# Indirect transfers spread over unit and expert steps, and two more slots turned by the transposing transfer, in a fused attention and mixture-of-experts kernel

## The chip, the cores and the metric

The kernel runs on one core of one Trainium2 chip. The metric is the time of the device in microseconds (us); lower is better.

## What is computed

Eight batches of 576 tokens with eight heads of 64 go through masked attention. The first four heads see a window of 32 tokens, the last four see every 32nd token. The result, 4608 tokens of 512 numbers, goes through a top-1 mixture of eight experts, each with a hidden layer of 1024. All numbers are float32.

```python
scores = scale * np.matmul(q, k.transpose(0, 1, 3, 2))
scores = np.where(masks, scores, -1e9)          # local for heads 0-3, strided for 4-7
attn = softmax(scores)
x = (attn @ v) as [4608, 512]
logits = x @ w_gate + modality_bias[modality_id]
e_idx = argmax(logits)
for e in range(8):
    h = np.maximum(x[e_idx == e] @ w1[e], 0.0)
    out[e_idx == e] = gate_w * (h @ w2[e])
```

## The kernel before, in words

**Attention, 0 to about 170 us.** Batches are taken in four pairs. Each pair has eight units, alternately a local head and a strided half, 32 units in all. A loop over n (line 1044) does one stage of several units in each turn: scores of unit n, transposes of n-2, masks of n+1, values of n-3. TensorE's order there is the order of the code. When a pair is complete, `finish_pair` and `route` (lines 465 to 605) turn its results, write the token rows to DRAM (`xd`), compute the router and write an entry for each token (`ld`), ordered by expert. They are generators, and `pop` runs five of their pieces per turn.

**Slots.** Tokens of one expert are handled in slots of 384. There are 12 slots that always run and one half slot. `slots(ph)` makes, on VectorE, tables of which rows belong to which slot (`li`, line 714) and which weights they need (`wi`, line 723). It runs three times, after the second, third and fourth pair. The first table serves slots 0 and 1, the second slots 2 and 3, the third slots 4 to 11.

**What a slot fetches.** Everything goes through GpSimd's (POOL's) indirect transfers, in POOL's order: three look-ups `le` (128 entries each, line 771), three gathers `fx` (128 token rows each, line 759), and the weights in four quarters of 1 MB (`raw0`, `raw1` and two in `raw23`, line 786); at the end three scatters `out` (line 938). A gather needs the look-up of its part, a look-up needs the table. `in_turn` (line 745) ties each of these behind the one before, so that the scheduler keeps the order of the code.

**What a slot computes.** `ffn` (line 907) runs eight steps f. A step casts the weights (`wh` on ScalarE line 951, `wl` on VectorE line 952), does 12 matmuls into `h` (line 916), a Relu (`hh`, line 919) and its remainder (`hl`, line 921), and two steps later 9 matmuls into `o` (line 930). Weights of the next slot are loaded at f = 1, 3, 5, 7 (`WHEN`). At f = 3 the look-ups of slot k+3 are issued, at f = 4 the gathers of slot k+2.

**Turning.** The gathered tokens have to be transposed. Slots 1 to 3 (below `TURNED`, line 47) get it from TensorE: 12 transposes at f = 4 of the slot before (`turn_tokens`, line 860). Slots from 4 on get it from the transposing transfer: at f = 1 VectorE splits the rows into 16-bit planes (`plane_tokens`, line 881), at f = 3 SyncE (SP) issues three transposing transfers (`send_tokens`, line 889), and at f = 6 VectorE puts the planes together (line 899) and ScalarE and VectorE make `xh` and `xl` (lines 903, 904). The three transposing transfers wait until quarter 1 of the next slot's weights has landed (line 892), and the first gather that comes after them waits until they have landed (line 763).

## Time and profile before

| | us |
|---|---|
| median of three runs | 617.81 (616.23 to 620.71) |
| the profiled execution, whole | 611.66 |
| its span, first to last instruction | 609.9 |
| TensorE busy in it | 577.3 |
| VectorE, ScalarE, GpSimd busy | 382.7, 328.3, 191.9 |
| mean granted TensorE clock | 0.979 of full |

The span is one execution; 1.76 us lie around it. "Idle" is the time that an engine stood before an instruction, and what follows the arrow is what ended it; "issue" means that nothing in the profile accounts for the wait. TensorE's clock has two levels, 1.2 and 2.4 GHz; 1.00 in the column PEclk is 2.4 GHz, 0.50 is 1.2 GHz.

### The profile page before, as it was taken

Reading aid. Unit: us, or ns where it says so; the run is one execution under the profiler, and the core shown is the slowest. Engines: PE = TensorE matmul, PEld = TensorE weight load, DVE = VectorE, ACT = ScalarE, POOL = GpSimd, SP = SyncE. Lnnn points to the kernel's source line nnn. Section 1 sums busy time; section 2 is a strip of 40 time slices with the busy share of each in tenths; the row PEclk is TensorE's granted clock in tenths of the full one; section 3 lists DMA queues with packets and bytes.
Section 4 is the critical chain, followed back from the end, with each engine's and each line's share of the span. In section 5 each row is a group of like instructions: output and inputs, shape, how many; then the busy total and the mean of one; then the engine's idle time right before and its main releaser. Section 6 shows DMA issues by size and latency. Waiting matters only on the chain.

```text
span 609.9 us, 13599 instructions
## 1 busy us (share of the span) xinstructions
PE 577.3 (95%) x5461; PEld 509.3 (84%) x5461; DVE 382.7 (63%) x925; ACT 328.3 (54%) x656; POOL 191.9 (31%) x184
## 2 busy tenths in 40 slices
PE   8789899878899999999999999999999999999995
PEld 5677778766778889899989999989989899989985
DVE  6775976863883777454666574747666666746432
ACT  5688887655682544453544453635445454536342
POOL 3010000044207132571444343352544534313211
PEclk9999999895999899999999999999999999999999
DMA  8997998887708422755363336550413345432511
GB/s 309 286 283 247 342 294 284 271 307 237 247 13 324 148 105 87 239 194 206 127 177 126 89 121 153 176 116 10 106 50 87 75 185 124 168 71 95 180 71 56
DMA packets 53723, 103.50 MB, mean 170 GB/s; under 512 B 32595, under 2 KB 32851, under 8 KB 49556
## 3 DMA queue, kind: packets, MB, share of 16 engines
q0 software_dynamic: 14592, 52.75, 25.3%
q1 hardware_dynamic: 33780, 39.85, 22.9%
q10 hardware_dynamic: 5280, 9.94, 4.7%
q8 instruction: 45, 0.74, 0.5%
q14 instruction: 26, 0.21, 0.1%
HBM read 98.28 MB, written 19.18 MB: 193 GB/s over the span
## 4 chain that ended last, share of the span: by engine, by line
PE 76%; issue 3%; ACT 1%; DVE 1%; POOL 0%; ACTq 0%; POOLq 0%
PE o L930 33%; PE h L916 33%; PE s L323 1%; PE ss L410 1%; PE o L358 1%; PE ot L455 1%; PE xs L217 1%; PE lg L504 1%; ACT wh L951 1%; PE xt L217 1%; PE ts L217 1%; PE en L600 1%; PE t L217 1%; PE hh L841 0%; PE xl L217 0%
## 5 line engine op out<-in xcount | busy, mean ns | idle before, releaser
L952 DVE TENSOR_TENSOR wl<-raw,wh 128x512 fp32r<-128x512 f32 x192 | 125.9, 694 | 91.1 <-ACT wh L951 72.9
L951 ACT CAST wh<-raw 128x512 fp32r<-128x512 f32 x192 | 109.3, 619 | 119.9 <-PE o L930 109.9
L916 PE MATMUL h<-xh,wl 128*128 128x384 f32 x384 | 129.5, 337 | 0.0
L916 PE MATMUL h<-xl,wh 128*128 128x384 f32 x384 | 129.0, 336 | 0.0
L916 PE MATMUL h<-xh,wh 128*128 128x384 f32 x384 | 128.1, 337 | 0.0
L930 PE MATMUL o<-wh,hl 128*128 128x512 f32 x288 | 114.3, 397 | 0.7 <-issue 0.7
L930 PE MATMUL o<-wl,hh 128*128 128x512 f32 x288 | 114.2, 397 | 0.3 <-issue 0.3
L930 PE MATMUL o<-wh,hh 128*128 128x512 f32 x288 | 113.4, 394 | 1.0 <-issue 1.0
L919 ACT ACTIVATE hh<-h 128x384 fp32r<-128x384 f32 x96 | 47.1, 491 | 88.2 <-PE h L916 75.1
L921 DVE SCALAR_TENSOR_TENSOR hl<-h,hh 128x384 fp32r<-128x384 f32 x96 | 53.3, 555 | 59.4 <-ACT hh L919 57.7
L786 POOL DMA_INDIRECT raw<-in_w,wi x48 | 60.7, 1264 | 70.4 <-DVE wl L952 38.6
L916 PEld LDWEIGHTS h<-xh,wh 128*128 128x128 f32 x384 | 72.2, 188 | 4.3 <-PE xs L217 0.4
L916 PEld LDWEIGHTS h<-xl,wh 128*128 128x128 f32 x384 | 72.1, 188 | 3.2
L916 PEld LDWEIGHTS h<-xh,wl 128*128 128x128 f32 x384 | 72.0, 188 | 0.0
L938 POOL DMA_INDIRECT out<-y,le x36 | 37.1, 1032 | 107.8 <-ACT y L937 103.5
L930 PEld LDWEIGHTS o<-wh,hl 128*128 128x128 f32 x288 | 54.4, 189 | 12.4 <-issue 0.9
L930 PEld LDWEIGHTS o<-wl,hh 128*128 128x128 f32 x288 | 54.3, 189 | 10.5 <-issue 1.2
L930 PEld LDWEIGHTS o<-wh,hh 128*128 128x128 f32 x288 | 54.5, 189 | 9.9 <-issue 0.9
L759 POOL DMA_INDIRECT fx<-xd,le x36 | 36.8, 1022 | 55.7 <-DMA work<-work 44.6
L771 POOL DMA_INDIRECT le<-ld,li x36 | 35.5, 987 | 40.6 <-DVE li L714 30.5
L594 POOL TENSOR_TENSOR hv<-hb,val 128x576 f32<-128x576 bf16 x4 | 5.1, 1282 | 83.6 <-DVE hb L585 46.1
L323 PE MATMUL s<-qk,qd 128*64 128x64 f32 x576 | 23.7, 234 | 6.9 <-issue 6.2
(191 smaller groups left out, 779.4 us busy)
## 6 DMA issues: line engine op xcount, KB each, us to landing
qk<-in_qkl SPq DMA_DIRECT2D x16, 592.0 KB
vv<-in_vl SPq DMA_DIRECT2D x16, 585.0 KB
qks<-in_qks SPq DMA_DIRECT2D x16, 576.0 KB
xd<-xt ACTq DMA_DIRECT2D x8, 1024.0 KB
vs<-in_vs SPq DMA_DIRECT2D x16, 288.0 KB
xd<-xt ACTq DMA_DIRECT2D x4, 256.0 KB
raw<-in_w,wi POOLq DMA_INDIRECT x48
le<-ld,li POOLq DMA_INDIRECT x36
```

The lines of the kernel that those rows point to most:

```text
L217: nc.tensor.transpose(dst, src, ident)
L323: nc.tensor.matmul(s[64 * jj:64 * jj + 64, g, :], qd[:, i, :, :].rearrange("p b q -> p (b q)"), qk[:, 18 + i:20 + i, :].rearrange("p b q - ...
L759: ins = in_turn(nc.gpsimd.indirect_dma_start(xt[:, h, :], None, xd[0:xrows, :], IOA(ap=le[:, h, 0:1], axis=0), **bounds))
L771: in_turn(nc.gpsimd.indirect_dma_start(le[:, h, :], None, ld[0:1 + last, :], IOA(ap=li[:, s, h:h + 1], axis=0)))
L786: ins = nc.gpsimd.indirect_dma_start(raws[j].rearrange("p f c -> p (f c)"), None, a["w"], IOA(ap=wi[:, s, j:j + 1], axis=0), bounds_check= ...
L916: nc.tensor.matmul(hp, w[:, a1], x[:, c, :], start=(k == 0), stop=(k == 11))
L919: nc.scalar.activation(hh[:], hp, AF.Relu)
L921: nc.vector.scalar_tensor_tensor(hl[:], hp, 0.0, hh.bitcast(F32), ALU.max, ALU.subtract)
L930: nc.tensor.matmul(os[h], hx[:, m], w[:, 512:1024], start=(f == 0 and i == 0), stop=(f == 7 and i == 2))
L938: outs.add(in_turn(nc.gpsimd.indirect_dma_start(out, IOA(ap=le[:, h, 0:1], axis=0), y[:], None, bounds_check=NT - 1, oob_is_err=False)))
L951: nc.scalar.copy(wh[:, c], raw[:, c])
L952: nc.vector.tensor_tensor(wl[:, c], raw[:, c], wh[:, c].bitcast(F32), ALU.subtract)
```

## The change

Each indirect transfer becomes a piece of its own. While attention runs, two pieces are issued per turn of the loop, once the first table is there; in the slots one piece per step. Each piece waits (a real wait) for a recent result, called its pace: in attention the last result of the values stage, in the slots the Relu of the step before. Scatters are no longer links of the chain. Slot 1 alone is turned by TensorE; slots 2 and 3 go through the transposing transfer as well.

```diff
-FIND, GATHER = 3, 4
-TURNED = 4
+TURNED = 2
...
-    def in_turn(ins):
+    def in_turn(ins, result=False):
         if ordered:
-            if ordered[-1]:
-                tc.add_manual_dep(ins.ins, ordered[-1], behind, reason="order of transfers")
-            ordered.append(ins.ins.name)
+            for name in ordered[-1][:1 if result else None]:
+                tc.add_manual_dep(ins.ins, name, behind, reason="order of transfers")
+            if result:
+                ordered[-1].append(ins.ins.name)
+            else:
+                ordered.append([ins.ins.name])
+            after_landing(ins, pace[-1])
         return ins
...
-                    for k in range(3):
-                        yield
-                        look_up(k)
-                    for k in range(2):
-                        yield
-                        gather(k)
-                    yield
-                    for j in range(2):
-                        weights(tables[0][1], 0, j, True)
...
+    for k in range(2):
+        fetch(k, look_up)
+        fetch(k, gather)
+        if k == 0:
+            queue.extend((0, partial(load, 0, j)) for j in range(4))
...
+        if 0 in tables:
+            if not ordered:
+                ordered.append([])
+            issue(2)
         if n == nu + 1:
             turn(0)
-            for j in (2, 3):
-                load(0, j)
...
-            if k == 0 and f == 0:
-                look_up(2)
-            if f == FIND:
-                look_up(k + 3)
-            if f == GATHER:
-                gather(k + 2)
-
+            issue(1 if f > 1 or (k == 0 and f) else 2 if k == 0 else 0)
+
+        if k == 0:
+            fetch(2, look_up)
+        fetch(k + 3, look_up, range(2))
+        fetch(k + 2, gather, range(1))
+        fetch(k + 3, look_up, range(2, 3))
+        fetch(k + 2, gather, range(1, 3))
```

In the rows that follow, the digit behind a name is the table, and the next one the slot of that table: `le2_0` is the look-up of slot 4, `fx1_1` the gather of slot 3, `h0_17` step 7 of slot 1, `h1_00` step 0 of slot 2.

GpSimd in the last third of attention, before: both first quarters of slot 0's weights, all look-ups and all gathers of slots 0 and 1 stand together.

```order
L786 DMA raw0_2515<-in_w,wi0_2389 128x2048
L786 DMA raw1_2519<-in_w,wi0_2389 128x2048
L771 DMA le0_0_2395<-ld_88,li0_2380 128x2 x3
L771 DMA le0_1_2399<-ld_88,li0_2380 128x2 x3
L759 DMA fx0_0_2493<-xd_87,le0_0_2395 128x512 x3
L759 DMA fx0_1_2504<-xd_87,le0_1_2399 128x512 x3
L786 DMA raw23_3294<-in_w,wi0_2389 128x2048 x2
L594 TENSOR_TENSOR hv2_3033<-hb2_3031,val2_2854 128x576
```

And in the changed kernel:

```order
L794 DMA le0_0_2395<-ld_88,li0_2380 128x2 x3
L777 DMA fx0_0_2489<-xd_87,le0_0_2395 128x512 x3
L809 DMA raw0_2728<-in_w,wi0_2389 128x2048
L809 DMA raw1_2732<-in_w,wi0_2389 128x2048
L597 TENSOR_TENSOR hv2_3028<-hb2_3026,val2_2839 128x576
L809 DMA raw23_2844<-in_w,wi0_2389 128x2048 x2
L794 DMA le0_1_2939<-ld_88,li0_2380 128x2 x3
L554 COPY val3_3511<-rt_sb_85 128x9
L777 DMA fx0_1_3031<-xd_87,le0_1_2939 128x512 x3
```

The weights of slot 0 moved behind its gathers, and the last two quarters and everything of slot 1 moved behind the router's product `hv2`.

GpSimd in slot 1, before: quarter 1 of slot 2's weights (`raw1` with `wi1`) stands ahead of the look-ups that need the third table `li2`.

```order
L786 DMA raw0_2515<-in_w,wi1_3225 128x2048
L938 DMA out_0<-y0_00_3928,le0_0_2395 4608x512
L938 DMA out_0<-y0_01_3933,le0_0_2395 4608x512
L938 DMA out_0<-y0_02_3938,le0_0_2395 4608x512
L786 DMA raw1_2519<-in_w,wi1_3225 128x2048
L771 DMA le2_0_4004<-ld_88,li2_3871 128x2 x3
L759 DMA fx1_1_4066<-xd_87,le1_1_3554 128x512 x3
L786 DMA raw23_3294<-in_w,wi1_3225 128x2048 x2
```

And in the changed kernel:

```order
L809 DMA raw0_2728<-in_w,wi1_3232 128x2048
L963 DMA out_0<-y0_00_3931,le0_0_2395 4608x512
L963 DMA out_0<-y0_01_3936,le0_0_2395 4608x512
L963 DMA out_0<-y0_02_3941,le0_0_2395 4608x512
L794 DMA le2_0_3969<-ld_88,li2_3871 128x2
L809 DMA raw1_2732<-in_w,wi1_3232 128x2048
L794 DMA le2_0_3969<-ld_88,li2_3871 128x2
L777 DMA fx1_1_4045<-xd_87,le1_1_3516 128x512
```

One look-up with `li2` now stands between the scatters and quarter 1.

VectorE in the changed kernel, from the Relu remainder of slot 1's step 6 to the tokens of slot 2 (`work1_0`, `xl1_0`):

```order
L946 SCALAR_TENSOR_TENSOR hl0_16_4115<-h0_16_4100,hh0_16_4113 128x384
L714 TENSOR_TENSOR row2_3859<-row2_3859,rt2_3860 128x60
L716 TENSOR_TENSOR rt2_3860<-r2_3857,sel2_3851 128x60
L717 SCALAR_TENSOR_TENSOR li2_3871<-row2_3859,rt2_3860 128x60
L977 TENSOR_TENSOR wl1_01_4208<-raw0_2728,wh1_01_4207 128x512 x2
L946 SCALAR_TENSOR_TENSOR hl0_17_4161<-h0_17_4146,hh0_17_4159 128x384
L977 TENSOR_TENSOR wl1_02_4261<-raw1_2732,wh1_02_4260 128x512 x2
L977 TENSOR_TENSOR wl1_03_4298<-raw1_2732,wh1_03_4297 128x512 x2
L922 COPY work1_0_3919<-work1_0_3919 128x1536 x2
L927 TENSOR_TENSOR xl1_0_4120<-work1_0_3919,xh1_0_4119 128x768 x2
```

Before, `li2` stood ahead of the remainder of step 5, and no `work1_0` was there.

## Rows read from the trace of the kernel before

**Rows 1.** Windows by stage: length; busy PE, PEld, DVE, ACT, POOL; PEclk; DMA; GB/s

```profile
134.00:140.00 6.00, 3.24 (x40) 2.15 (x38) 0.51 (x2) 1.30 (x3) 2.88 (x4) 0.79 0.45 171
140.00:154.00 14.00, 12.28 (x167) 10.59 (x165) 5.44 (x22) 8.34 (x20) 6.00 (x6) 0.50 0.88 295
196.00:203.00 7.00, 5.01 (x15) 3.44 (x14) 2.52 (x5) 3.17 (x8) 1.81 (x2) 0.76 0.71 227
203.00:317.00 114.00, 114.00 (x602) 103.45 (x601) 71.65 (x162) 53.30 (x99) 44.95 (x41) 1.00 0.46 152
317.00:551.00 234.00, 234.00 (x1178) 212.30 (x1177) 149.83 (x211) 114.46 (x204) 94.72 (x85) 1.00 0.40 113
```

**Rows 2.** Chain that ended last, two slot boundaries: start us, us, what

```profile
350.32 4.12 PE o L930 x18
...
383.75 4.12 PE o L930 x18
```

**Rows 3.** TensorE's waits, 126 to 204 us: in total, times, longest

```profile
PE ss L410 <- issue: 2.8, 5, 1.2
PE s L323 <- issue: 2.6, 5, 1.0
PE o L930 <- issue: 2.0, 3, 1.0
```

**Rows 4.** Timeline of TensorE: start, us, instruction, idle before it

```profile
128.36 0.30 PE L217 MATMUL ts<-cf_sb,ens 128*72 128x128 f32 x1 [1.51 <-issue]
...
199.09 0.59 PE L930 MATMUL o<-wl,hh 128*128 128x512 f32 x1 [0.30 <-issue]
...
202.46 0.40 PE L930 MATMUL o<-wh,hh 128*128 128x512 f32 x1
```

**Rows 5.** Timeline of GpSimd, weights, look-ups and gathers

```profile
126.56 1.23 POOL L786 DMA_INDIRECT raw<-in_w,wi  x1 [12.20 <-DVE tk L738]
128.09 1.00 POOL L786 DMA_INDIRECT raw<-in_w,wi  x1 [0.31 <-DMA vs<-in_vs]
...
163.40 1.15 POOL L594 TENSOR_TENSOR hv<-hb,val 128x576 f32<-128x576 bf16 x1 [4.29 <-DVE hb L585]
...
228.57 1.05 POOL L786 DMA_INDIRECT raw<-in_w,wi  x1 [0.30 <-DVE wa L723]
240.74 0.98 POOL L771 DMA_INDIRECT le<-ld,li  x1 [11.12 <-DVE li L714]
242.03 0.94 POOL L771 DMA_INDIRECT le<-ld,li  x1 [0.31 <-issue]
...
297.39 1.04 POOL L786 DMA_INDIRECT raw<-in_w,wi  x1 [0.30 <-issue]
...
309.90 0.94 POOL L759 DMA_INDIRECT fx<-xd,le  x1 [7.68 <-DMA work<-work]
```

**Rows 6.** Timeline of SyncE, the transposing transfers for slot 4

```profile
303.16 4.12 SPq L889 DMA_TRANSPOSE work<-work  x3
```

**Rows 7.** Timeline of VectorE, the third table and slot 4's tokens

```profile
240.25 0.21 DVE L714 SCALAR_TENSOR_TENSOR li<-row,rt 128x60 int32<-128x60 f32 x1
...
292.81 3.40 DVE L881 COPY work<-fx 128x1536 uint16<-128x1536 uint16 x2
...
313.27 0.56 DVE L921 SCALAR_TENSOR_TENSOR hl<-h,hh 128x384 fp32r<-128x384 f32 x1 [0.68 <-issue]
313.74 1.99 DVE L899 COPY work<-work 128x1536 uint16<-128x1536 uint16 x2
...
316.82 1.81 DVE L904 TENSOR_TENSOR xl<-work,xh 128x768 fp32r<-128x768 f32 x2
```

**Rows 8.** Timeline of ScalarE, two casts

```profile
199.83 1.14 ACT L951 CAST wh<-raw 128x512 fp32r<-128x512 f32 x2 [5.17 <-remote]
...
315.88 1.57 ACT L903 CAST xh<-work 128x768 fp32r<-128x768 f32 x2
```

**Rows 9.** Chain that ended last, TensorE's transposes for slot 3

```profile
269.59 1.31 PE xt L217 x12
```

More of the change, by code (lines that the diff above doesn't have):

```diff
@@ L260, in attention_moe, with mark @@
     outs = _Group(tc, "outs")
+    pace = [None]
+    def mark(ins):
+        pace.append(ins)
     ap_cm = tc.tile_pool(name="ap", bufs=1)
@@ L743, in attention_moe, with after_landing, token_parts @@
     behind = mybir.DependencyInfo(mybir.DependencyClass.NoSync, mybir.DependencyReason.DATA)
-    def in_turn(ins):
+    landed = mybir.DependencyInfo(mybir.DependencyClass.Sync, mybir.DependencyReason.DATA)
+    def after_landing(ins, other):
+        tc.add_manual_dep(ins.ins, other.ins.name, landed, reason="transfers kept apart")
+    def in_turn(ins, result=False):
         if ordered:
-            if ordered[-1]:
-                tc.add_manual_dep(ins.ins, ordered[-1], behind, reason="order of transfers")
-            ordered.append(ins.ins.name)
+            for name in ordered[-1][:1 if result else None]:
[5 more added lines that the diff above has]
+            after_landing(ins, pace[-1])
         return ins
     def tokens(n, le, xrows):
+        parts = token_parts(n, le, xrows)
+        for _ in range(TH):
+            got = next(parts)
+        return got
+    def token_parts(n, le, xrows):
         xt = pre.tile([P, TH, DM], F32, tag="fx", name=f"fx{n}")
@@ L763, in tokens, with entry_parts @@
                     after_landing(ins, t)
-        return xt, le
+            yield xt, le
     def entries(n, li, s, xrows):
+        for le in entry_parts(n, li, s, xrows):
+            pass
+        return le
+    def entry_parts(n, li, s, xrows):
         le = pre.tile([P, TH, 2], I32, tag="le", bufs=5, name=f"le{n}")
@@ L772, in entries @@
                 le[:, h, :], None, ld[0:1 + last, :], IOA(ap=li[:, s, h:h + 1], axis=0)))
-        return le
+            yield le
     raws = {}
@@ L853, in half_ffn @@
         outs.add(in_turn(nc.gpsimd.indirect_dma_start(
-            out, IOA(ap=le[:, 0, 0:1], axis=0), y[:], None, bounds_check=NT - 1, oob_is_err=False)))
+            out, IOA(ap=le[:, 0, 0:1], axis=0), y[:], None, bounds_check=NT - 1, oob_is_err=False), True))
     def parts_of(n, odd):
@@ L905, in split_tokens @@
         return xh, xl, le
+    steps = []
     def ffn(fp, n, xh, xl, le, between, load=None):
@@ L918, in up @@
             hh = fp.tile([P, SLOT], F32R, tag="hh", bufs=3, name=f"hh{n}{f}")
-            nc.scalar.activation(hh[:], hp, AF.Relu)
+            steps.append(nc.scalar.activation(hh[:], hp, AF.Relu))
             hl = fp.tile([P, SLOT], F32R, tag="hl", bufs=3, name=f"hl{n}{f}")
@@ L938, in finish @@
                 outs.add(in_turn(nc.gpsimd.indirect_dma_start(
-                    out, IOA(ap=le[:, h, 0:1], axis=0), y[:], None, bounds_check=NT - 1, oob_is_err=False)))
+                    out, IOA(ap=le[:, h, 0:1], axis=0), y[:], None, bounds_check=NT - 1, oob_is_err=False), True))
         def down_last(*args):
@@ L952, in ffn @@
                 nc.vector.tensor_tensor(wl[:, c], raw[:, c], wh[:, c].bitcast(F32), ALU.subtract)
+            if steps:
+                mark(steps[-1])
             if load and f in WHEN:
@@ L999, in attention_moe @@
             plan.append((f"{ph}_{i}", ph, i, NT + 1 if last else (bp + 1) * T2))
-    landed = mybir.DependencyInfo(mybir.DependencyClass.Sync, mybir.DependencyReason.DATA)
     quarter, turning = {}, []
-    def after_landing(ins, other):
-        tc.add_manual_dep(ins.ins, other.ins.name, landed, reason="transfers kept apart")
     def load(k, j):
@@ L1011, in load @@
             quarter[j] = weights(tables[plan[k][1]][1], plan[k][2], j)
-    found, gathered, sent, turned = {}, {}, {}, {}
+    found, gathered, sent, turned, parts = {}, {}, {}, {}, {}
     def look_up(k):
@@ L1017, in look_up, with fetch, issue @@
             found[k] = half_entries()
-        if k < len(plan) and plan[k][1] in tables:
+        elif k < len(plan):
             n, t, s, xrows = plan[k]
-            found[k] = entries(n, tables[t][0], s, xrows)
+            if ("le", k) not in parts:
+                parts["le", k] = entry_parts(n, tables[t][0], s, xrows)
+            found[k] = next(parts["le", k])
     def gather(k):
-        if k not in found:
-            look_up(k)
         if k == len(plan):
             gathered[k] = half_tokens(found[k])
-        if k < len(plan):
-            gathered[k] = tokens(plan[k][0], found[k], plan[k][3])
+        elif k < len(plan):
+            if ("fx", k) not in parts:
+                parts["fx", k] = token_parts(plan[k][0], found[k], plan[k][3])
+            gathered[k] = next(parts["fx", k])
+    queue = []
+    def fetch(k, what, h=range(TH)):
+        for i in h:
+            if k < len(plan) or (k == len(plan) and i == 0):
+                queue.append((k, partial(what, k)))
+    def issue(count):
+        for _ in range(count):
+            if queue and (queue[0][0] >= len(plan) or plan[queue[0][0]][1] in tables):
+                queue.pop(0)[1]()
     def turn(k):
```

8 lines of the change are left out of this document (3 added, 5 removed).

## Prediction, made before the changed kernel was run

> **What bounds the kernel now.** I read the windows by stage first, because the mean shares mix attention with slots. From 317 to 551 us TensorE is busy 234.00 of 234.00 us at full clock, and from 203 to 317 us 114.00 of 114.00 [rows 1]. Two boundaries in the chain give the length of a slot: 383.75 - 350.32 = 33.43 us, so 4.18 per step [rows 2]. In these stretches a transfer that comes sooner buys nothing, and a change helps only by taking work off TensorE.
>
> What is lost lies at two other places, which the windows with a low busy share or clock, the waits and the timeline show.
>
> - *The last part of attention, 126 to 160 us.* Waits put down to "issue" are 2.8 + 2.6 us [rows 3], and one of 1.51 stands at 128.36 [rows 4]. The clock is 0.79 over 3.24 us of work and 0.50 over 12.28 us of work [rows 1], which costs 3.24 x 0.21 + 12.28 x 0.50 = 6.8. Together 13.7 us. The first weights go out at 126.56 and 128.09 [rows 5], and the DMA share reaches 0.88 in the slow stretch [rows 1].
> - *Slot 0, 196 to 203 us.* TensorE works 5.01 of 7 us, at 0.76 [rows 1]: 2.0 idle and 7 x 0.24 = 1.7 of clock, 3.7 us. The idle part is the 2.0 before `o` [rows 3]; one of its pieces is at 199.09 [rows 4]. ScalarE too stood 5.17 us before a cast there, ended by "remote", which is none of its engines [rows 8].
>
> So 17.4 us could be won from spreading, no more, unless attention itself gets shorter.
>
> **What TURNED = 2 takes from TensorE.** Twelve transposes at 1.31 us [rows 9], for slots 2 and 3. Both stand in the stretch in which TensorE never idles, so all of it counts: 2 x 1.31 = 2.6 us off. In return VectorE gets 3.40 + 1.99 us per slot [rows 7], twice. It is busy 71.65 of 114 us there [rows 1], so 10.8 more fit; I cost them at nothing, hidden by the matmuls of the steps that they stand in. If that cover were gone, a step would be late by at most the 3.40 of its planes, twice 6.8; that is the other end, and below nothing I see no way.
>
> **The new wait between slots 1 and 2.** This is the main cost. The transposing transfers of a slot wait for its quarter 1. Before, quarter 1 of slot 2 was issued at 228.57, some 12 us ahead of the look-ups that need the third table; the look-up at 240.74 had waited 11.12 us for `li` [rows 5]. Now one of these look-ups stands ahead of quarter 1, and GpSimd works in order. `li2` itself has moved behind the remainder `hl` of step 6 of slot 1. Let E be the end of the h matmuls of step 7 of slot 1. Step by step:
>
> - `hl` of step 6 starts when the h of that step ends, at E - 4.18, and takes 0.56 [rows 7]; three small operations of the kind of `li` (0.21 [rows 7]) follow: the table is there at about E - 2.5, with gaps of an estimated half microsecond.
> - The look-up runs about 0.3 later, as before (240.25 + 0.21 to 240.74), and the next transfer 1.29 after it (242.03 - 240.74) [rows 5]: quarter 1 is issued at E - 0.9.
> - For slot 4 the transposing transfers began 303.16 - 297.39 = 5.77 us after quarter 1 was issued [rows 5, 6]: E + 4.9.
> - The first gather behind them ran at 309.90, 6.74 after their start, and had waited for them [rows 5]: landed at E + 11.6.
> - VectorE puts planes together in 1.99, then ScalarE's cast (1.57 for two) and the remainder (1.81 for two) [rows 7, 8] have to begin: half of them is enough to start the h matmuls: E + 11.6 + 2.0 + 0.8 + 0.9, about E + 15. The `wl` of steps 2 and 3, which stand on VectorE before it, need quarter 1 only, at E + 5, and are done by then.
>
> TensorE has only the rest of slot 1 behind E: 27 matmuls of `o`, 4.12 x 27 / 18 = 6.2 us [rows 2]. In the order of the changed kernel no work of slot 2 comes that does not need these tokens. So it idles about 15 - 6.2 = 9 us. After a pause the clock was 0.76 over 7 us [rows 1], which gives another 1.7. I take 10.7. Queued behind the waiting look-up on GpSimd are quarter 1, two more look-ups, the gathers of slot 3 and the last two quarters; the last are needed only 4 steps into slot 2 (16.7 us) and so stay covered. Bounds: 6, if the table is made two microseconds earlier and the clock does not fall; 14, if transposing beside a quarter of 1 MB takes 3 us longer.
>
> **Spreading in attention.** The changed order issues look-ups and gathers of slot 0 alone first, then two quarters; the other two quarters and all of slot 1 stand behind `hv2`, which ran at 163.40 [rows 5]. So about half of the bytes leave the stretch with the losses. The gate remains the table, so the three look-ups and three gathers still go out in groups, and the first two quarters now come near 140 us, into the stretch at half clock. I give back 5 of 13.7. Bounds: all 13.7; or -2, if the quarters at 140 meet the token writes that are made there and new gaps come.
>
> **Spreading in the slots.** The quarters of slot 0 that were late are not the reason for the idle 2.0 (that wait is "issue", not data), but the transfers before it were together. I give 2.5 of 3.7; bounds 0 and 3.7. The real waits on the Relu of the step before hold GpSimd at most one step, 4.18, with 16 us of lead on weights: nothing. If that lead were gone, a late quarter would cost one step.
>
> By the Trainium skill ("Runtime: NRT & Kernel Launch", section "Instruction fetch mechanics") an engine's instructions are refilled in blocks by a DMA queue of their own, and crossing a block is mostly hidden. The waits "issue" of [rows 3], which nothing else ends, come where DMA is busy and would fit a refill that is held up; if instead it stays hidden, as the page has it, spreading would return none of the 5.4 + 1.5 us there. The rivals R1 and R2 below stand on the rows alone.
>
> **The sum**, against the profiled execution of 611.66: -2.6 (transposes) + 10.7 (wait) - 5 (attention) - 2.5 (slot 0) = +0.6, so 612.3. The median of the timed runs is 617.81, 6.15 above this execution, and no row shows where. If it sits in the same gaps, spreading wins 7.5 of 17.4 of it too, 2.6; if not, nothing. That is 615.8 to 618.4; I take 617. Its own range, with the wait at 6 to 14, is 612 to 622.
>
> **Rivals.**
>
> - *R1, faster: bursts make all the losses.* Then 17.4 goes: 611.66 + 10.7 - 2.6 - 17.4 = 602.4, with 6.15 on it 608.5. For it: gaps without a cause that begin within two microseconds of the first weight transfers [rows 4, 5], and ScalarE stopped at the same time as TensorE in slot 0. Against: the groups of three and the quarters at 140 remain.
> - *R2, slower: the wait at slot 2 stands and spreading wins nothing.* The gaps move, or come from something else (how long TensorE idled before the clock fell). 611.66 + 10.7 - 2.6 = 619.8, with 6.15 it is 625.9. It decides from the point where the wait is more than what spreading and the missing transposes return, 2.6 us with nothing won. For it: the change in GpSimd's order keeps the same bytes; the low clock may follow from attention's own thin work at 134 to 140 (3.24 of 6 us).
> - *R3, the wait at slot 2 does not come.* If the table were ready two steps earlier, quarter 1 would be too, and only gains are left: 611.66 - 2.6 - 7.5 = 601.6, with 6.15 it is 607.7. For it: in the kernel before the table was there at 240.5 [rows 7], some 9 us before the end of slot 1's h (three slots before the boundary at 350.32 [rows 2], about 250). Against: VectorE's new order, with `li2` behind the remainder of step 6.
> - *R4, it does not do what it says.* The scheduler could leave the transfers together; the order of the changed kernel shows them apart in the slots and in two groups in attention, so this is R2 in another dress and has no chance of its own.
>
> **How the numbers follow.** Forecast 0.47, R1 0.26, R2 0.20, R3 0.07. One per cent is 6.2 us, about what a measurement of this kernel can tell from no change. R1 and R3 are faster by over that: 0.33. The forecast is within 1%: 0.47. R2 is slower: 0.20. The range goes from 605, some 3 us under R1 and R3, to 628, some 2 over R2. Where the losses go in whole and the wait is also at its lower bound it would be 603.8, which is left out with part of R1.
>
> **What would show it.** Right: a single wait of TensorE, 7 to 11 us, just before the first h of slot 2, ended by `xh` or `xl`; behind it on VectorE the put-together that waits for SyncE's transfers; on GpSimd a look-up that waits for `li` ahead of quarter 1; no 12 transposes in slots 1 and 2; fewer "issue" waits at 126 to 160 and at 196 to 203, with less time at 0.50. Wrong: no idle time of more than 3 us there (R3); no "issue" waits left and the clock full from 140 on (R1); as many of them as before, later (R2); or a new wait in a steady slot, where I have none.

## The result, and the profile after

| | before | after |
|---|---|---|
| median, 20 runs each | 616.32 (609.57 to 620.71) | 619.50 (614.33 to 623.78) |
| the profiled execution | 611.66 | 617.37 |
| its span | 609.9 | 615.4 |

The ratio after / before is 1.0068, with a 95% interval of 1.0039 to 1.0097. The change loses about 4.2 us (0.0068 x 616.3). The ratio leaves out the slowest runs of each kernel, so it is not the ratio of the two medians, which differ by 3.2 us. The forecast of 617 from 617.81 was a gain of 0.8; the time lies in its range, the sign does not fit.

The windows of the changed kernel, same columns as [rows 1]:

```profile
134.00:140.00 6.00, 3.72 (x55) 2.77 (x45) 0.52 (x2) 1.55 (x3) 4.76 (x5) 1.00 0.31 84
140.00:154.00 14.00, 11.79 (x196) 10.05 (x194) 6.12 (x25) 7.58 (x18) 2.16 (x3) 0.63 0.95 329
196.00:203.00 7.00, 7.00 (x41) 6.20 (x39) 5.76 (x14) 4.82 (x12) 3.37 (x3) 1.00 0.81 292
240.00:270.00 30.00, 22.30 (x106) 20.03 (x105) 13.71 (x25) 10.82 (x20) 11.41 (x11) 0.89 0.55 162
317.00:551.00 234.00, 234.00 (x1178) 212.29 (x1178) 149.88 (x211) 114.80 (x204) 99.43 (x89) 1.00 0.41 117
```

Three things are to be seen. Slot 0 (196 to 203) is full now: 7.00 of 7.00 at full clock, against 5.01 at 0.76. From 240 to 270, where TensorE never idled before, it works 22.30 of 30. And 134 to 154 still has its idle time and low clock (0.63 for 0.50).

The hole from 240 to 270 is one wait. These are lines of the timeline of the changed kernel on GpSimd, SyncE, VectorE, ScalarE and TensorE around it:

```profile
243.16 0.22 DVE L717 SCALAR_TENSOR_TENSOR li<-row,rt 128x60 int32<-128x60 f32 x1
...
243.65 0.99 POOL L794 DMA_INDIRECT le<-ld,li  x1 [17.61 <-DVE li L717]
244.94 1.04 POOL L809 DMA_INDIRECT raw<-in_w,wi  x1 [0.31 <-ACT wh L976]
...
257.47 1.40 POOL L777 DMA_INDIRECT fx<-xd,le  x1 [10.22 <-DMA work<-work]
...
250.76 4.10 SPq L912 DMA_TRANSPOSE work<-work  x3
...
256.83 1.92 DVE L922 COPY work<-work 128x1536 uint16<-128x1536 uint16 x2 [2.95 <-DMA work<-work]
...
258.78 1.56 ACT L926 CAST xh<-work 128x768 fp32r<-128x768 f32 x2 [4.14 <-DVE work L922]
...
251.13 0.84 PE L955 MATMUL o<-wh,hl 128*128 128x512 f32 x3
259.67 1.33 PE L941 MATMUL h<-xh,wh 128*128 128x384 f32 x3 [7.70 <-ACT xh L926]
```

Read it from the top: the table `li` at 243.16 lets the look-up go, the look-up lets quarter 1 (`raw`) go, its landing lets the transposing transfers go at 250.76, their landing lets VectorE put planes together, then ScalarE casts, and TensorE, which had run out of `o` at 251.97, starts again at 259.67.

The rest of the loss is harder to see, because it is a move. In the kernel before, TensorE went from the matmuls `en` of the third pair to the first h of slot 0 without a gap:

```profile
164.61 1.20 PE L600 MATMUL en<-hv,ha 128*36 128x64 f32 x18 [0.65 <-POOL hv L594]
...
171.55 0.42 PE L916 MATMUL h<-xh,wh 128*128 128x384 f32 x1
```

In the changed kernel the same instructions have gaps in between, and GpSimd is issuing there what the change put behind `hv`:

```profile
162.51 1.20 PE L603 MATMUL en<-hv,ha 128*36 128x64 f32 x18 [0.69 <-POOL hv L597]
...
166.20 0.22 PE L361 MATMUL o<-vv,et 128*64 128x65 f32 x1 [0.36 <-issue]
...
168.36 0.49 PE L216 MATMUL xt<-cf_sb,fx 128*128 128x128 f32 x3 [0.77 <-issue]
...
169.80 0.73 PE L458 MATMUL ot<-eb,vs 72*64 72x72 f32 x15 [0.74 <-issue]
...
174.52 0.45 PE L941 MATMUL h<-xh,wh 128*128 128x384 f32 x1
...
162.61 1.03 POOL L809 DMA_INDIRECT raw<-in_w,wi  x1 [0.15 <-issue]
163.94 1.00 POOL L809 DMA_INDIRECT raw<-in_w,wi  x1 [0.30 <-issue]
165.25 0.97 POOL L794 DMA_INDIRECT le<-ld,li  x1 [0.30 <-issue]
166.52 0.95 POOL L794 DMA_INDIRECT le<-ld,li  x1 [0.30 <-issue]
167.78 0.95 POOL L794 DMA_INDIRECT le<-ld,li  x1 [0.30 <-issue]
```

From `en` to h it is 171.55 - 164.61 = 6.94 before and 174.52 - 162.51 = 12.01 after. At the start of `en` the changed kernel was 2.10 us ahead; at the first h it is 2.97 behind. The windows of just these two stretches, before and after (columns as in [rows 1]), show what the 5.1 us are made of:

```profile
164.61:171.55 6.94, 6.94 (x118) 6.35 (x118) 6.28 (x30) 5.35 (x12) 0.19 (x1) 1.00 0.19 58
162.51:174.52 12.01, 9.70 (x118) 8.40 (x118) 6.72 (x30) 6.34 (x14) 7.15 (x8) 0.86 0.57 196
```

TensorE stands idle for 12.01 - 9.70 = 2.3 us (1.9 of it "issue"), and the same 118 matmuls take 9.70 us for 6.94, at a granted clock of 0.86 for 1.00.

### The profile page after: what moved, and what is told of

Read it like the earlier page. It is cut to its first block, busy times and chain, and to the rows that moved or that the text cites. A ratio compares the mean times of both kernels' runs of the same rounds, so it can differ in the third digit from the quotient of the medians.

```text
span 615.4 us, 13581 instructions
## 1 busy us (share of the span) xinstructions
PE 577.1 (94%) x5437; PEld 509.1 (83%) x5437; DVE 392.9 (64%) x929; ACT 327.8 (53%) x652; POOL 192.9 (31%) x184
## 4 chain that ended last, share of the span: by engine, by line
PE 72%; DVE 4%; issue 3%; DMA 1%; ACT 1%; POOL 0%; SPq 0%; ACTq 0%; POOLq 0%; DVEq 0%
PE h L941 32%; PE o L955 31%; PE o L361 1%; PE s L326 1%; DMA raw<-in_w,wi 1%; PE xs L216 1%; PE ot L458 1%; PE ss L413 1%; PE xt L216 1%; PE lg L507 1%; PE t L216 1%; PE en L603 1%; DVE wl L977 1%; DMA work<-work 1%; PE hh L864 0%
## 5 line engine op out<-in xcount | busy, mean ns | idle before, releaser
L955 PE MATMUL o<-wh,hl 128*128 128x512 f32 x288 | 113.0, 395 | 0.0
L777 POOL DMA_INDIRECT fx<-xd,le x36 | 39.3, 1093 | 98.4 <-DMA work<-work 41.5
L794 POOL DMA_INDIRECT le<-ld,li x36 | 37.5, 1043 | 55.1 <-issue 19.6
L904 DVE COPY work<-fx 128x1536 uint16<-128x1536 uint16 x20 | 34.1, 1745 | 7.2 <-DMA fx<-xd,le 6.1
```

The costliest lines, as they stand in the source:

```text
L777: ins = in_turn(nc.gpsimd.indirect_dma_start(xt[:, h, :], None, xd[0:xrows, :], IOA(ap=le[:, h, 0:1], axis=0), **bounds))
L794: in_turn(nc.gpsimd.indirect_dma_start(le[:, h, :], None, ld[0:1 + last, :], IOA(ap=li[:, s, h:h + 1], axis=0)))
L904: pin(nc.vector.tensor_copy(rows[:, :, w, :], halves(xt)[:, :, :, w]))
L955: nc.tensor.matmul(os[h], hx[:, m], w[:, 512:1024], start=(f == 0 and i == 0), stop=(f == 7 and i == 2))
```

## The experiments

The kernel before takes 616 to 620 us in some sessions and 602 in others, so ratios are compared between runs of like sessions. One trace is one execution, and its first part, up to about 110 us, scatters by some 6 us (107.97 to 114.18 below). To compare traces I cut each at five instructions of TensorE that every kernel has: the 1236th matmul of the scores (counted from 0), the first `en` of the third pair, and the first h of slots 0, 1 and 4.

The letters of the runs: a, spreading alone; b, the transposing transfer alone; c, quarter 1 ahead of the look-up; e, as c with slot 1's look-ups and gathers moved into slot 0; f, as c with no indirect transfer in attention; g, as e with look-ups set apart by quarters; h, as e with the transfers paced in pairs; i, as h with single gathers. "Again" and "third" are repeats. Lengths in us:

| kernel (session by the kernel before) | to scores | to `en` | to slot 0 | slot 0 | slots 1 to 3 | rest |
|---|---|---|---|---|---|---|
| before (616) | 108.27 | 56.33 | 6.94 | 42.90 | 106.41 | 289.01 |
| before_again (616) | 109.73 | 59.56 | 6.94 | 41.25 | 106.41 | 289.08 |
| after (616) | 109.42 | 53.10 | 12.00 | 38.34 | 113.32 | 289.27 |
| after_again (616) | 112.09 | 52.03 | 12.19 | 38.83 | 114.14 | 289.11 |
| after_third (618) | 110.37 | 54.96 | 12.30 | 38.89 | 114.33 | 289.06 |
| c_again (616) | 107.97 | 54.47 | 12.01 | 38.27 | 105.29 | 289.18 |
| f_none_in_attention (616) | 112.95 | 45.55 | 22.17 | 40.33 | 104.99 | 289.16 |
| e_third (618) | 114.14 | 53.65 | 7.69 | 39.04 | 105.54 | 289.12 |
| h_again (618) | 110.89 | 52.90 | 8.32 | 38.80 | 104.94 | 289.05 |
| h_third (620) | 113.43 | 50.55 | 8.07 | 39.03 | 106.48 | 289.09 |
| i_single (620) | 110.88 | 45.32 | 10.53 | 38.31 | 110.16 | 289.15 |
| a_spread_alone (602) | 112.52 | 48.68 | 7.25 | 38.76 | 106.44 | 289.42 |
| b_transposing_alone (602) | 112.82 | 46.37 | 9.26 | 38.76 | 103.77 | 289.45 |
| c_quarter_first (602) | 113.31 | 42.30 | 6.94 | 38.74 | 103.98 | 289.56 |
| e_again (602) | 110.51 | 42.63 | 6.95 | 38.82 | 103.74 | 289.02 |
| h_paced (602) | 111.04 | 43.37 | 6.94 | 38.95 | 103.74 | 289.17 |
| a_again (602) | 111.95 | 46.38 | 8.31 | 38.89 | 106.44 | 289.13 |
| e_slot1_later (602) | 109.19 | 44.99 | 6.94 | 38.82 | 103.73 | 289.14 |
| g_lookups_apart (602) | 114.18 | 50.38 | 8.33 | 38.83 | 103.73 | 289.32 |

**Each half of the change alone.** The changed kernel with the old limit (spreading alone), and the kernel before with the new one.

```diff
-TURNED = 2
+TURNED = 4
```

> The changed kernel with TURNED = 4: the transfers are spread, slots 2 and 3 are turned by TensorE as before. My theory (spreading wins about 4.4 us in slot 0, nothing on balance in attention because the 'issue' waits move from 126-160 us to 162-171 us; the wait at the start of slot 2 belongs to the transposing transfer alone): 616.3 - 4.4 + 1 = 613, between 611 and 615; no wait over 1 us of TensorE before the first h of slot 2; the first h of slot 0 at 172 to 176 us. Rival 1 (spreading wins the 5 us in attention that I forecast and the profiled execution hid it): 607 to 608, first h of slot 0 below 168. Rival 2 (the late quarter 1 itself holds slot 2 up): 617 to 622 with an idle time of 4 us or more in step 2 of slot 2.

```diff
-TURNED = 4
+TURNED = 2
```

> The kernel before with TURNED = 2: slots 2 and 3 by the transposing transfer, transfers bunched as before; quarter 1 of slot 2 still goes out ahead of the look-ups that need the third table. My theory (the wait comes from the order of quarter 1 and that look-up alone): no wait of TensorE over 1 us before the first h of slot 2, the transposing transfers for slot 2 more than 5 us before the end of slot 1's h; 616.3 - 2.6 = 613.7, between 612 and 615. Rival (transposing so early in the slots costs by itself: planes on VectorE, or transfers beside the look-ups): an idle time of 5 us or more before slot 2, 620 or more.

Spreading alone: 598.93 against 602.41, ratio 0.9958 (0.9921 to 0.9994), no wait before slot 2 (the traced execution, 604.94, was the longest of the twelve). So it gained 2.5 us, where I expected 3 and rival 1 expected 9. The transposing transfer alone: 601.87, ratio 1.0002 (0.9965 to 1.0039). Its trace has no wait before slot 2, and slots 1 to 3 take 103.77, which is 2.64 less than 106.41, as the two sets of transposes ask for. The total does not show that gain. Two losses stand in its trace that neither trace of the kernel before has: `en` waits 2.94 us for `hv` (0.65 before), and from `en` to slot 0 it takes 9.26 us for 6.94, at a granted clock of 0.72 for 1.00. No trace of the kernel before was taken in a session of 602, so whether these are the transposing transfer's doing is open. What both runs settle: neither half has the wait; it needs both, the look-up ahead of quarter 1 and tokens that come behind quarter 1. Spreading alone came out again as

> Spreading alone (TURNED = 4) again. My theory, where the kernel before takes about 616: slot 0 gains 4 us, attention nothing on balance (12 us between the en of the third pair and the first h, 52 to 54 before it), ratio 0.990 to 0.997; the changed kernel's 1.003 to 1.007 less the wait of 9.4 and plus the transposes of 2.6 is 0.992 to 0.996, the same. Rival (spreading wins nothing): 0.998 or more.

That session was again one of 602, not 616: ratio 0.9945 (0.9917 to 0.9972), 598.43 against 602.35. It gains 2.5 to 3.3 us there; in a session of 616 it was not run. Its order of transfers is that of the changed kernel, yet from `en` to slot 0 it takes 7.25 and 8.31, not 12: the loss there belongs to the sessions of 616.

**Quarter 1 ahead of the look-up.** In slot 1 the first look-up of slot 4 is issued one step later.

```diff
-            issue(1 if f > 1 or (k == 0 and f) else 2 if k == 0 else 0)
+            issue({2: 0, 3: 2}.get(f, int(f > 1)) if k == 1 else 1 if f > 1 or (k == 0 and f) else 2 if k == 0 else 0)
```

> The changed kernel, but in slot 1 the first look-up of slot 4 is issued one step later, behind quarter 1 of slot 2; nothing else differs. My theory: the 7.7 us of idle time before the first h of slot 2 and some 1.7 us of lower clock behind it go, 619.5 - 9.4 = 610, between 608 and 612. Rival (the wait was set by the tokens of slot 2 or by VectorE, and the look-up only stood in front of it): at least 4 us of idle time stay, 615 or more.

> The kernel with quarter 1 first, unchanged, timed again on the chip of the changed kernel. My theory: 8 to 10 us below the changed kernel of the same call, no wait before the first h of slot 2. Rival (its gain was the spread in attention on that chip): less than 4 us below the changed kernel.

> The changed kernel, unchanged, timed beside the kernel with quarter 1 first. My theory: the wait of 7 to 8.5 us before the first h of slot 2 is there on any chip; the kernel with quarter 1 first is 1.3 to 1.7 per cent (8 to 10 us) faster than this one. Where the kernel before takes about 602, this one takes 0.3 to 1.0 per cent more, since it loses 9.4, wins 2.6 and finds little in slot 0 to win. Rival (the changed kernel's loss came from attention on the first chip alone): it is faster than the kernel before here.

In the first session (602) the ratio was 0.9927 (0.9889 to 0.9965). Beside the changed kernel, in a session of 616: 610.29 against 619.01, ratios 0.9914 (0.9877 to 0.9950) and 1.0030 (0.9998 to 1.0062). The medians differ by 8.7, the ratios by 1.16% or 7.1 us, against 8 to 10 expected; in the traces slots 1 to 3 are 114.14 - 105.29 = 8.9 shorter. The timeline of the kernel with quarter 1 first shows why: quarter 1 goes out 20 us before the look-up that waits, and the transposing transfers are done long before slot 1 ends.

```profile
226.21 1.04 POOL L809 DMA_INDIRECT raw<-in_w,wi  x1 [0.30 <-issue]
246.35 2.31 POOL L794 DMA_INDIRECT le<-ld,li  x1 [19.09 <-DVE li L717]
...
231.88 4.10 SPq L912 DMA_TRANSPOSE work<-work  x3
```

The rival (tokens or VectorE) falls: the late table is still late (the look-up waits 19.09 us), and TensorE does not wait for it.

**A second trace of the kernel before.**

> The kernel before, unchanged, for a second trace beside the ones of this call. The four runs above ran where the kernel before takes 602 us, 14 us less than where the two kernels were first timed. My theory (the 'issue' waits in pieces of eight instructions at 134 to 139, 147 to 149 and 197 to 199 us are what differs, since none of the four traces shows them): where the time is near 602, the part from the first h of slot 0 on is 434 to 436 us instead of 438.3, with no 'issue' wait in slot 0, and 'issue' waits stand in attention only where a block of 256 instructions begins; where it is near 616, they are all there again. Rival (another cause, such as slower transfers throughout): the part from the first h of slot 0 on differs by less than 1 us.

614.88 us, so this was a session of 616, and the waits are there again: in slot 0 (41.25 instead of 38.8) and from 137 to 149 us.

**Where the "issue" waits in attention come from.** First I took every indirect transfer out of attention, in the kernel with quarter 1 first; slot 0 has to start late by that.

```diff
-            issue(2)
+            issue(8 if n >= nu else 0)
```

> The kernel with quarter 1 first, and no indirect transfer is issued before the last two turns of attention: slot 0's look-ups, gathers and weights come late on purpose. My theory (look-ups and gathers issued in a row make the waits 'issue' in pieces where the chip shows them, the bursts of weights lengthen those at the blocks): between the 1236th score and the matmuls en of the third pair 41 to 43 us, against 56.3 (before) and 53.1 (changed) on the first chip and 42 to 49 in the four runs; then slot 0 begins late by 5 to 12 us, which gives it all back and more. Rival (attention's own order makes the waits, whatever GpSimd does): that stretch as long as in the changed kernel of this call, within 2 us.

The waits of TensorE from 130 to 160 us, in total, times and longest, in the kernel before of that session, in the changed one, and in this one:

```profile
PE s L323 <- issue: 5.5, 6, 1.1
PE t L217 <- issue: 2.0, 2, 1.0
```

```profile
PE s L326 <- issue: 3.9, 7, 0.9
PE ts L216 <- issue: 1.5, 1, 1.5
```

```profile
PE ts L216 <- issue: 0.7, 1, 0.7
PE ot L458 <- ACT eb L448: 0.7, 1, 0.7
PE rk L563 <- DVE xt L374: 0.4, 1, 0.4
```

The waits before the scores `s` are gone, and the stretch up to `en` is 45.55 instead of 52.03 to 59.56 (54.47 with quarter 1 first and the transfers in place, c_again, in the same session). So they are not attention's own; they come with GpSimd's transfers. In this kernel three of them stand at 176.81, 178.21 and 178.91 us, where the transfers stand now. The 45.55 is above the 41 to 43 that I expected. Its total, 0.9959 (0.9921 to 0.9998), has the lateness of slot 0 in it (22.17 for 6.94).

Next I left slot 0's transfers where they are and moved the look-ups and gathers of slot 1 out of the end of attention into slot 0.

```diff
-    for k in range(2):
+    for k in range(1):
         fetch(k, look_up)
         fetch(k, gather)
...
-            issue(1 if f > 1 or (k == 0 and f) else 2 if k == 0 else 0)
+            issue(2 if k == 0 else {2: 0, 3: 2}.get(f, int(f > 1)) if k == 1 else int(f > 1))
...
         if k == 0:
+            fetch(1, look_up)
+            fetch(1, gather)
             fetch(2, look_up)
```

> As the kernel with quarter 1 first, and the look-ups and gathers of slot 1 are not issued at the end of attention but in the first steps of slot 0, two transfers per step. My theory (the 'issue' waits of TensorE stand behind three or more look-ups in a row, wherever they are put): the waits that the changed kernel has at 164 to 171 us are gone, the first h of slot 0 comes about 10 us or less behind the 18 matmuls en of the third pair instead of 12.0, (6.9 in the kernel before), and the time is 2 to 5 us below that of the kernel with quarter 1 first: 605 to 608, if slot 0 gets no new waits. Rival 1 (they stand behind the weights, whose quarters 2 and 3 stay there): the waits at 164 to 171 stay, no gain. Rival 2 (bursts in slot 0 cost as much there): as many 'issue' waits in slot 0, no gain.

> The kernel with quarter 1 first and slot 1's look-ups and gathers moved into slot 0, timed again. My theory, where the kernel before takes about 616: the part from the matmuls en of the third pair to the first h of slot 0 is 7 us instead of the changed kernel's 12, so the time is 4 to 5 us below the 0.991 of the kernel with quarter 1 first, a ratio of 0.983 to 0.987, if slot 0 stays at 38 to 39 us. Rival (weights make the waits at 164 to 171): 12 us there and 0.991.

> Quarter 1 first and slot 1's look-ups and gathers moved into slot 0, a third time. Where the kernel before takes about 616 (the chips that show TensorE's 'issue' waits in pieces): my theory (they follow the indirect transfers) says 7 us from the en of the third pair to the first h instead of 12, and a ratio of 0.981 to 0.987; rival (weights alone make them): 12 us and 0.991. Where it takes about 602: 0.990 to 0.993 as before.

In what follows, waits in pieces are "issue" waits of TensorE that come close together, with a handful of instructions between them; the last section shows some. In the two sessions of 602 there were none to remove, and the ratios, 0.9928 (0.9884 to 0.9971) and 0.9907 (0.9871 to 0.9943), are near the 0.9927 of the kernel with quarter 1 first. In the session of 618 it is 608.01, ratio 0.9832 (0.9781 to 0.9883), and the end of attention has no "issue" wait any more:

```profile
167.79 1.20 PE L603 MATMUL en<-hv,ha 128*36 128x64 f32 x18 [0.68 <-POOL hv L597]
...
175.49 0.45 PE L941 MATMUL h<-xh,wh 128*128 128x384 f32 x1 [0.19 <-ACT wh L976]
...
167.89 1.03 POOL L809 DMA_INDIRECT raw<-in_w,wi  x1
169.22 1.00 POOL L809 DMA_INDIRECT raw<-in_w,wi  x1 [0.30 <-issue]
```

It takes 7.7 us from `en` to h instead of the changed kernel's 12.3 in the same session. The two quarters are still there, so here two quarters alone do not make the waits; in the kernel before a pair of them (156.82 and 158.12) has two short ones behind it, 0.47 and 0.43 us. The waits behind slot 0's own look-ups and gathers stay (53.65).

Then I tried what in such a run does it: look-ups set apart by quarters, and transfers paced in pairs.

```diff
-    for k in range(2):
-        fetch(k, look_up)
-        fetch(k, gather)
-        if k == 0:
-            queue.extend((0, partial(load, 0, j)) for j in range(4))
+    for h in range(TH):
+        fetch(0, look_up, range(h, h + 1))
+        if h < 2:
+            queue.append((0, partial(load, 0, h)))
+    fetch(0, gather)
+    queue.extend((0, partial(load, 0, j)) for j in (2, 3))
```

> As the kernel before this in the list, but in attention each look-up of slot 0 is followed by a quarter of weights, so that no two look-ups stand in a row; the gathers stay in a row. My theory (look-ups in a row starve TensorE of instructions): the 'issue' waits of about 1 us at instructions 5530 to 5590 go, the stretch from the 1236th score to the en of the third pair is 43 to 48 us instead of 52 to 56, and the ratio is 0.970 to 0.980. Rival 1 (any run of six or more indirect transfers does it): that stretch stays at 52 to 56. Rival 2 (the gathers do it): the waits come later, behind the gathers, and are as long.

```diff
-            issue(2)
+            issue(2 if n >= 27 else 0)
```

> As the first in this list, but attention issues no transfer before turn 27, two per turn from there, each pair behind the newest result of the values: the transfers are in fact spread over attention, which the changed kernel's waits do not do, since the results they wait for are old when the table comes. My theory: no two pairs stand closer than 3 us, the 'issue' waits in pieces go, 43 to 47 us from the 1236th score to the en of the third pair, slot 0 starts without waiting for its tokens; ratio 0.965 to 0.978. Rival (a look-up alone is enough): the waits are there after each pair, stretch 50 to 56.

> Transfers really paced in attention (two per turn from turn 27), again. Where the kernel before takes about 616: my theory (three or more look-ups in a row make the waits) says no 'issue' waits in pieces, 43 to 47 us from the 1236th score to the en of the third pair instead of 52 to 56, ratio 0.965 to 0.978; rival (each look-up or gather makes them, however far apart): 50 to 56 us, 0.98 or more. Where it takes about 602: 0.992 to 0.998 as before.

> The paced kernel a third time, beside the one with single gathers. My theory, where the kernel before takes about 616: waits in pieces only behind the run of two gathers and two quarters, as in the trace before this one (152 to 157 us); ratio 0.972 to 0.983, slower than the one with single gathers by 4 us or more. Rival: the two within 2 us.

The first of the two ran in a session of 602 alone, so it says nothing on the pieces; it lost (1.0050, 1.0016 to 1.0085), with one wait of 5.05 us for `hv`: on GpSimd `hv` stood behind two quarters of weights, the first of which had waited 8.11 us for its pace, a result of ScalarE (161.03). Pacing in pairs gave 0.9943 (0.9906 to 0.9979) at 602, and 0.9773 (0.9723 to 0.9823) and 0.9811 (0.9752 to 0.9869) at 618 and 620. But my reason for it fell, and the stretch up to `en` is 52.90 and 50.55 us at 618 and 620, not 43 to 47. No waits follow the pairs of look-ups at 134.84 and 136.31; they follow the run of two gathers and two quarters, with no look-ups in a row at all. Timeline of the paced kernel, GpSimd and three of seven waits on TensorE:

```profile
151.35 1.00 POOL L777 DMA_INDIRECT fx<-xd,le  x1 [4.48 <-DVE xt L374]
152.66 1.00 POOL L777 DMA_INDIRECT fx<-xd,le  x1 [0.30 <-issue]
153.96 1.00 POOL L809 DMA_INDIRECT raw<-in_w,wi  x1 [0.30 <-issue]
155.26 1.00 POOL L809 DMA_INDIRECT raw<-in_w,wi  x1 [0.30 <-issue]
...
153.43 0.28 PE L413 MATMUL ss<-qks,qz 128*36 128x18 f32 x2 [0.52 <-issue]
154.19 0.33 PE L413 MATMUL ss<-qks,qz 128*36 128x18 f32 x3 [0.48 <-issue]
154.94 0.38 PE L413 MATMUL ss<-qks,qz 128*36 128x18 f32 x6 [0.43 <-issue]
```

So I set the gathers apart too.

```diff
-    for k in range(2):
-        fetch(k, look_up)
-        fetch(k, gather)
-        if k == 0:
-            queue.extend((0, partial(load, 0, j)) for j in range(4))
+    fetch(0, look_up)
+    queue.append((0, partial(load, 0, 0)))
+    fetch(0, gather, range(2))
+    queue.append((0, partial(load, 0, 1)))
+    fetch(0, gather, range(2, 3))
+    queue.extend((0, partial(load, 0, j)) for j in (2, 3))
...
-            issue(2)
+            issue({27: 2, 28: 2, 29: 1, 30: 2}.get(n, int(n > 30)))
```

> As the paced kernel, but gathers of slot 0 go one per turn or beside one quarter only, and a quarter stands behind the look-ups: no three indirect transfers in a row before the matmuls en of the third pair. My theory (runs of three or more look-ups, gathers or both make TensorE's waits in pieces on the chips that show them): where the kernel before takes about 616, no 'issue' waits in pieces, 44 to 48 us from the 1236th score to the en of the third pair, ratio 0.962 to 0.972. Rival (single gathers make them as well): waits of together 3 us or more behind the gathers, 50 us or more, ratio 0.975 to 0.985. Where it takes about 602: no such waits in any kernel, 0.990 to 1.000.

The waits in pieces are gone from attention, but for a single one of 0.40 at 144.66, and the stretch is 45.32, as without any transfers (45.55). The total is 0.9763 (0.9696 to 0.9829), above the 0.962 to 0.972 that I expected (it falls in the rival's range, without the rival's waits) and not told apart from the paced one (605.60 against 606.95). It gives back what it wins: the last gather is late (a wait of 1.8 us for `fx`), and in slots 2 and 3 there are "issue" waits of 4.3 us. Two of them, at 263.26 and 264.70, come behind fifteen transfers in a row from 242.83 to 262.07, which GpSimd issues because the late third table had held it up for 23 us; the one of 3.1 at 297.34 comes behind thirteen more (275.31 to 295.44), but as one long wait and not in pieces, so what made it is open:

```profile
PE o L955 <- issue: 3.6, 2, 3.1
PE h L941 <- issue: 0.7, 1, 0.7
```

**The changed kernel a third time.**

> The changed kernel again, beside these. Where the kernel before takes about 602 and has no waits in pieces: it loses 9.4 - 2.6 = 6.8 at slot 2, and what spreading wins there is what the kernel with spreading alone won (0.9945 and 0.9958, 2.5 to 3.3 us): ratio 1.004 to 1.009. Where it takes about 616: 1.000 to 1.008. Rival (the wait at slot 2 is shorter there): 1.000 or less.

The session was one of 618: ratio 1.0058 (1.0014 to 1.0102), with the wait of 7.80 before slot 2. The changed kernel was never timed in a session of 602. An estimate of its ratio there: 0.9927 for the kernel with quarter 1 first, and the 8.9 us of slots 1 to 3 on top, 8.9 / 602 = 0.0148, make about 1.007.

## Why the prediction was wrong

The sum had four terms. Against the two traces of the kernel before and the three of the changed one, all from sessions of 616 to 618 (means of the table; the first column, +1.6, is scatter of the same code and is left out):

| term | forecast | measured | how |
|---|---|---|---|
| transposes and the wait at slot 2 | -2.6 + 10.7 = +8.1 | +7.5 | slots 1 to 3: 113.93 - 106.41 |
| slot 0 | -2.5 | -3.4 | 38.69 - 42.08 |
| attention, up to `en` | -5 | -4.6 | 53.36 - 57.95 |
| attention, `en` to slot 0 | not in the sum | +5.2 | 12.16 - 6.94 |
| sum | +0.6 | +4.7 | ratio 1.0068: +4.2; medians: +3.2 |

**The wait at slot 2: right, step by step.** E, where slot 1's last h ends and the next `o` starts, was 245.65. The table was there at 243.38, E - 2.3 (forecast E - 2.5); quarter 1 was issued at E - 0.7 (E - 0.9); the transposing transfers began at E + 5.1 (E + 4.9) and had landed by 256.83, E + 11.2 (E + 11.6); the first h came at E + 14.0 (E + 15). The idle time was 7.7 for 9. With the 2.6 of the transposes taken back, the table's +7.5 makes the whole wait, lower clock included, 10.1 for 10.7. Putting quarter 1 first removed it, which shows the cause.

**TURNED = 2: right.** Slots 1 to 3 are 2.64 shorter where nothing else is changed there (b_transposing_alone; 2.67 against a_spread_alone of the same session). The planes on VectorE cost nothing that a trace shows.

**Slot 0: right in sign, undersized.** It is full in the changed kernel; 3.4 of the 3.7 that I had counted came, for the 2.5 that I gave. In a session of 602 there was nothing to win: with the old order slot 0 takes 38.76 there too (b_transposing_alone).

**Attention: this step failed.** What was expected of the old place came, 4.6 us for 5, though not by fewer waits:

```profile
126.00:160.00 34.00, 26.92 (x443) 21.83 (x439) 16.29 (x71) 18.04 (x43) 15.93 (x16) 0.75 0.76 261
126.00:160.00 34.00, 27.76 (x540) 22.54 (x539) 19.24 (x89) 19.85 (x48) 8.08 (x8) 0.85 0.75 251
```

From 126 to 160 us, before and after, the "issue" waits are 6.9 and 6.1 us, and it is the granted clock that rose, from 0.75 to 0.85. Half of the indirect transfers did leave the stretch (GpSimd has 8 instructions there for 16), but the DMA engines are as busy as before (0.75 for 0.76, 251 GB/s for 261). So "about half of the bytes leave the stretch with the losses" is not shown as the reason, and that the size came out is in part luck. The step that failed is the other end. I wrote that "the other two quarters and all of slot 1 stand behind `hv2`", took that only as bytes that leave, and set nothing against it at the new place. There, on a stretch in which TensorE had no idle time before, the run of transfers brought "issue" waits and a lower clock, 5.2 us together. My lower bound of +2 for new gaps had them at 140 us, where the quarters meet the token writes; the loss stood at 164 to 171. R2 had said it in words ("the gaps move") and had the right sign; at 625.9 on the median shown it gave slot 0 no gain, and so was too high. Moving slot 1's look-ups and gathers away took 12.3 to 7.7 in the same session, which shows this; with quarter 1 first alone it stays 12.01 (c_again). In sessions of 602 the stretch has no such waits, with slot 1's transfers in it or not.

**The sentence on the Trainium skill** ("Runtime: NRT & Kernel Launch", section "Instruction fetch mechanics") left open whether a refill of instructions is hidden. The Trainium skill has the crossing from one block to the next as mostly hidden. The traces agree in part: of 19 such crossings in attention, 7 have a wait, of 0.6 to 2.9 us, as the last section shows. But of the 5.4 + 1.5 us that the sentence was about, only the 1.5 at 128.36 stand at such a place; the 5.4 come in pieces and away from these places.

**The base.** The sum was +0.6, a loss; that the forecast was a gain of 0.8 came from the base, of which spreading was to win about half of 2.6 us, if the 6.15 us between the median and the profiled run sat in the same gaps. No run shows that term. I counted on a median of 617.81; over 20 runs it is 616.32, so 1.5 of the 6.15 was the small sample. The own range, 612 to 622, stands on two footings (617 - 4.7 and 618.4 + 3.3); from 615.8 to 618.4 it would be 611 to 622.

## What to carry to other kernels

When a change moves transfers, charge each of them at the place where it arrives, by what the same transfers cost where they stood; here 4.6 us were won at the old place and 5.2 lost at the new one. A wait that is tied to an old result paces nothing: the changed kernel's transfers wait for results of the values, but the table that they all need comes later than these, so they leave in one run. On an engine that works in order, look what waits longest, and see what the change has put behind it: one look-up of 128 entries ahead of a quarter of weights cost 10 us, and one step's shift in the order gave 7 to 9 back.

## What the runs showed that I had not expected

TensorE's "issue" waits are of two kinds. The first stand at fixed places. I counted TensorE's records (matmuls, weight loads, its sequencer's) from the start: such waits come before record 705, 961, 1986, 3265, 4289, 4546 and 5314, in the first trace of the kernel before and in that of the changed one alike. The distances from 705 are 256, 1281, 2560, 3584, 3841 and 4609: multiples of 256, within one. From 705 to 5313 there are 19 such places; at the other 12 TensorE's matmuls have no such wait over 0.25 us. In the page's list of queues the instruction queue moves 0.74 MB in 45 packets, 16.4 KB each (columns: packets, MB, share of the engines' time):

```profile
q8 instruction: 45, 0.74, 0.5%
```

In both traces each of these waits ended 1.2 to 1.8 us after one of the packets was through. 1.51 us at 128.36 [rows 4] is one: its packet ran from 125.90 to 126.82. So in attention, where TensorE goes through 256 such records in about 6 us (5313 in the first 126.85) and the DMA share is 0.8 to 1.0, a refill is not always hidden; in the slots of these two traces, where a step of 4.18 us has 42 of them and 256 take 25 us, no such wait is seen. That the packet was late because of the other transfers is likely and was not tested.

The second kind comes in pieces. Here are weight loads of TensorE in the changed kernel (after_again), one line for each piece:

```profile
139.15 0.21 PEld L326 LDWEIGHTS s<-qk,qd 128*64 128x64 f32 x4 [0.48 <-issue]
139.86 0.13 PEld L326 LDWEIGHTS s<-qk,qd 128*64 128x64 f32 x1 [0.51 <-issue]
140.57 0.24 PEld L326 LDWEIGHTS s<-qk,qd 128*64 128x64 f32 x4 [0.58 <-issue]
142.00 0.39 PEld L326 LDWEIGHTS s<-qk,qd 128*64 128x64 f32 x5 [1.19 <-issue]
143.45 0.33 PEld L326 LDWEIGHTS s<-qk,qd 128*64 128x64 f32 x4 [1.05 <-issue]
```

They start every 0.71 us or twice that, with a handful of loads each, while the DMA engines are far from full (DMA share 0.51 from 139 to 144 in this trace, 0.31 from 134 to 140 in the first one). But for one or two waits of 0.4 to 0.5 us behind a pair (158.85 and 159.58 in the kernel before, 128.26 in before_again, 147.41 in h_again, 148.22 in h_third, 144.66 in i_single), they begin in or behind runs of four or more indirect transfers that are issued 0.3 us behind one another, and not every run makes them: seven in a row from 185.77 us on, in slot 0 of the changed kernel, made none. All traces from sessions of 616 to 620 have them and none from sessions of 602, and for kernels that were traced in both this stretch is most of the difference (up to `en` 54.47 against 42.30 with quarter 1 first, 53.65 against 42.63 with slot 1 moved, 52.90 against 43.37 for the paced one). What differs between the sessions, and by what way a run of GpSimd's transfers holds up TensorE's instructions, stays open. The record has chip number 11 for a session of 602 and for one of 620, so, if that number means the same chip, it is not a fixed trait of a chip.

Quarter 1 first has a price of this kind too. Behind the late third table GpSimd then issues fifteen transfers in a row, from 246.35 to 266.08 in c_again, and waits in pieces stand behind them (the longest, 0.71, at 268.18); slots 1 to 3 take 105.29 us there, and 103.98 in a session of 602.

The two best versions, the paced one and the one with single gathers, take 0.976 to 0.981 of the kernel before in sessions of 616 to 620; in one of 602 the paced one takes 0.994, and slot 1 moved with quarter 1 first 0.991 to 0.993. All beat the kernel before; beside the changed kernel (621.67) the paced one (604.57) and slot 1 moved (608.01) ran in one session and beat it too.
